# Two chained FFNs behind a recurrence: the 64-row matmul of the K = 320 remainder widened to 128 rows, and a re-scaled emission clock

## The chip, the cores and the metric

One core of one Trainium2 chip. The metric is device time in microseconds (us) of one execution. PE is TensorE (PEld its weight loads), DVE VectorE, ACT ScalarE, POOL GpSimd, SP SyncE.

## The reference, cut to what matters

A recurrence over 768 steps gives 3072 tokens of 320 numbers (the kernel's first 600 us; the change does not touch it). Then a router gives each token one of 8 experts (384 places each, greedily by the highest score), and two FFNs follow:

```python
for e in range(E):                       # E = 8, 384 tokens each
    h = np.maximum(x[mask] @ w1[e], 0.0) # [384, 320] @ [320, 1024]
    out[mask] = h @ w2[e]                # [384, 1024] @ [1024, 320]
h = x @ w_in                             # [3072, 320] @ [320, 2048]
g = h * np.clip(h + 3.0, 0.0, 6.0) / 6.0
return g @ w_out                         # [3072, 2048] @ [2048, 320]
```

## The kernel before, in words

**Stages.** `attention` is the recurrence. `moe` then does, for each of 8 experts in an order found at run time, both FFNs for its 384 tokens: 8 `hstage` (first FFN in, one 128-wide block of F1 each) with 8 `ystage` (first FFN out) two blocks behind, then 16 `gstage` (second FFN in) with 16 `ostage` (second FFN out) two blocks behind. The last two `ostage` of an expert, the scaling and the three scatters are done as `tails` between the first blocks of the next expert.

**Precision.** Every operand is a pair of float32r tiles, `h` (rounded) and `l` (what was lost). A product is h·h + l·h + h·l. `proj` (line 1091) does one block of the contraction over 320 for `hstage` and `gstage`: rows 0 to 127 (k = 0), 128 to 255 (k = 1), and the rest of 64 rows (k = 2). For the rest, one tile `x2` (or `y2`) holds h in its partitions 0 to 63 and l in 64 to 127, and the high weights `wh[2]` hold the same 64 rows twice, so that one matmul on 128 rows does h·h and h·l. A second matmul, on 64 rows, does l·h: `wl[2][0:64]` by `x2[0:64]`. So `proj` is 8 matmuls, in the order k = 0 (three), k = 2 (two), k = 1 (three), one 64-row matmul among seven on 128 rows; there are 8 + 16 blocks in each of 8 experts, 192 in all. In the page they are all line 1053 (`mm`), and the weights tell them apart: `x,w1l` and `y,win_l` are the 64-row ones.

**What sets the order.** Each engine runs its instructions in the order in which the program emits them. The routing of the next expert (`routing`, `place`, `xt`) is a set of Python generators that runs in between: `mm` emits a matmul and then calls `tick(n / 2400)`, with n its columns, so 0.16 for 384 columns and 0.133 for 320. This is the emission clock. A `yield r` in a generator means: go on when the clock has run r + PACE further (0.7). `later(us, f)` puts small steps (`gl` of a block, a weight DMA) off by so much of the clock. No time of the chip enters: if a DVE answer is not there when PE reaches the matmul that reads it, PE waits.

**The routing of an expert**, on DVE and PE by turns: six rounds of a search (DVE masks L774 and L776, 24 small matmuls L779, compare L793, matmul L796 on 8 rows, count L800); then matmuls L823 to L825, DVE, L840 and L841, then DVE L844 to L854, which end with `r_cb` (L852), and the matmuls L857 and L859 on `r_cb`, with `yield 1.8` between; then `place` (L907, L928) and `xt` (L1067).

**Other names.** `ph` is the PSUM tile of a projection (two of them, by turns), freed in `hstage` by DVE's `gl` (L1132) and in `gstage` by DVE's `gt` (L1206). POOL does the low parts (`w1l`, `w2b`, `w2c`, the second FFN's `gl`) and issues the gathers and scatters.

Of the kernel before, what the change touches and what calls it, by code (L numbers as in the profile page):

```python
# [18 lines left out]
F32, F32R, BF, I32 = mybir.dt.float32, mybir.dt.float32r, mybir.dt.bfloat16, mybir.dt.int32  # L19
AF = mybir.ActivationFunctionType  # L20
OP = mybir.AluOpType
# [583 lines left out]
E, CAP, NT, N = 8, 384, 24, 3072  # L605
DM, F1, F2 = 320, 1024, 2048
BIG = 1.0e38
PACE = 0.7
DVN, DVP = 4, 0
PACE1 = 0.3  # L610
NPRE = 8
# [18 lines left out]


def decoder(nc, raw_in, pool, wd):
    """One piece of w_in and w_out: from the float64's two words to the nearest float32."""
    V, A, P_, SY = nc.vector, nc.scalar, nc.gpsimd, nc.sync
    raws = {}

    def fetch(n):
        raw = raws[n] = pool.tile([128, 256, 2], I32, name="d_raw", bufs=2)
        SY.dma_start(raw.rearrange("p a b -> p (a b)"), raw_in[n].bitcast(I32))

    def head(n):
        raw = raws[n]
        w, lo = raw[:, :, 1], raw[:, :, 0]
        t = pool.tile([128, 256], I32, name="d_t", bufs=1)
        V.tensor_scalar(t, w, 3, 0x3ffffff8, op0=OP.logical_shift_left, op1=OP.bitwise_and)
        hf = pool.tile([128, 256], I32, name="d_hf", bufs=1)
        V.scalar_tensor_tensor(hf, w, -(1 << 30), t, op0=OP.bitwise_and, op1=OP.bitwise_or)
        raws[n] = (w, t, hf, lo)

    def scale(n):  # L650
        w, ex, hf, lo = raws[n]
        lf = pool.tile([128, 256], F32, name="d_lf", bufs=1)
        A.mul(lf, lo.bitcast(mybir.dt.uint32), 2.0 ** -52)
        sp = pool.tile([128, 256], I32, name="d_sp", bufs=1)
        V.tensor_scalar(sp, hf, -(1 << 23), None, op0=OP.bitwise_and)
        V.tensor_scalar(ex, w, 20, 0x7ff, op0=OP.logical_shift_right, op1=OP.bitwise_and)
        raws[n] = (ex, hf, sp, lf)

    def add(n):
        ex, hf, sp, lv = raws[n]  # L660
        E = P_ if n % DVN < DVP else V
        E.tensor_mul(lv, lv, sp.bitcast(F32))
        E.tensor_add(lv, lv, hf.bitcast(F32))
        raws[n] = (ex, lv)

    def value(n):
        ex, lv = raws.pop(n)
        v = pool.tile([128, 256], F32, name="d_v", bufs=2)
        V.scalar_tensor_tensor(v, ex, 896.5, lv, op0=OP.is_ge, op1=OP.mult)
        SY.dma_start(wd[:, 256 * n:256 * n + 256], v)  # L670

    return NP, fetch, head, scale, add, value


def moe_consts(nc, per, io):
    """Constants and state of the routing: the tiles, and what fills them."""
    V, P_, SY = nc.vector, nc.gpsimd, nc.sync
    k = {}
    for n, shape, dt in (("rc", [128, 242], F32), ("iota", [128, 128], BF), ("io4", [128, 16], BF), ("io5", [128, 32], BF), ("io6", [128, 64], BF), ("iot", [128, 3], BF), ("ones", [128, 128], BF), ("tri", [128, 128], BF),
                         ("tri1", [128, 128], BF), ("rst", [128, E * NT], F32), ("asg", [128, NT, E], F32), ("unas", [128, NT], F32),  # L680
                         ("act", [128, E], F32), ("capb", [128, E], F32), ("q", [128, E], F32), ("q8", [128, 1], F32),
                         ("spacer", [128, 1], F32), ("three", [128, 1], F32)):
        k[n] = per.tile(shape, dt, name=n)
    rc = k["rc"]
    k["prefw"] = rc[:, 0:192].rearrange("p (j e) -> p j e", j=NT)
    k["jp"] = rc[:, 192:240].rearrange("p (j c) -> p j c", j=NT)
    k["pcol"] = rc[:, 240:241]

    def io_(n, w, base=0):
        P_.iota(k[n], pattern=[[1, w]], base=base, channel_multiplier=0, allow_small_or_imprecise_dtypes=True)  # L690

    fill = [lambda: SY.dma_start(rc, io["rc"]), lambda: io_("iota", 128), lambda: io_("iot", 3, -8)]
    fill += [lambda n=n, v=v: P_.memset(k[n], v) for n, v in (("ones", 1.0), ("rst", 1.0), ("asg", 0.0), ("unas", 1.0), ("act", 1.0), ("capb", BIG),
                                                             ("q", float(CAP)), ("q8", float(CAP)), ("three", 3.0))]
    fill += [lambda: P_.memset(k["rst"].rearrange("p (e j) -> p e j", e=E)[:, :, 0:1], 0.0)]
    fill += [lambda b=b: P_.tensor_scalar(k[f"io{b}"], k["iota"][:, :1 << b], 0.5 ** b, None, op0=OP.mult) for b in (4, 5, 6)]
    fill += [lambda: V.tensor_scalar(k["tri"], k["iota"], k["pcol"], None, op0=OP.is_gt),
             lambda: V.tensor_scalar(k["tri1"], k["iota"], k["pcol"], None, op0=OP.is_ge)]

    return k, fill  # L700


def moe(tc, nc, io, cst, xd, LG, wd, out):
# [5 lines left out]
    V, A, P_, T_, SY = nc.vector, nc.scalar, nc.gpsimd, nc.tensor, nc.sync  # L709
    ident = cst["ident"]  # L710
    k = cst["k"]
# [6 lines left out]
    def rt(shape, dtype, name, bufs=1):  # L718
        return wk.tile(shape, dtype, name="r_" + name, bufs=bufs)
# [3 lines left out]
    def routing(ph, vbits):  # L723
        S3, S2 = [128, NT, E], [128, NT]
        if ph < E - 1:
# [10 lines left out]
            s = rt(S2, I32, "s")  # L736
# [26 lines left out]
            for i, (sh, b) in enumerate(vbits):  # L763
# [16 lines left out]
                if i:  # L780
                    t = rt(S2, F32, "dp")
                    V.tensor_scalar(t, z, cnt, None, op0=OP.subtract)
                else:
                    t = z
# [67 lines left out]
            V.tensor_copy(cb, cn)  # L852
            V.tensor_sub(unas, unas, sel)
            V.tensor_add(asg, asg, oa)  # L854
            yield 1.8
            pn = ps.tile([128, 512], F32, name="pn")
            T_.matmul(pn[:, 0:E], ones, cb, start=True, stop=True)  # L857
            pc = ps.tile([128, 512], F32, name="pc")
# [83 lines left out]
        res[ph]["xg"] = xg  # L942
        yield XG

# [1 line left out]
    def stage(name):  # L946
        return wk.tile([128, 1024], F32, name="stg", bufs=2)

# [2 lines left out]
    wo_h = per.tile([128, 16, DM], F32R, name="wo_h")  # L951
    wo_l = per.tile([128, 16, DM], F32R, name="wo_l")

    def split(hi, lo, src, leng, rows=128):
        A.copy(hi, src)
        leng.tensor_tensor(lo[0:rows], src[0:rows], hi[0:rows].bitcast(F32), OP.subtract)

    rest = []

    def load_win():  # L960
        wh, wl = wo_h.rearrange("p k n -> p (k n)"), wo_l.rearrange("p k n -> p (k n)")
        cuts = [(win_h[:, k], win_l[:, k], 2048 * k, 1024 * c, 1024, k) for k in range(2) for c in range(2)]
        k2 = [(win_h[:, 2], win_l[:, 2], 4096, 1024 * c, 1024, 2) for c in range(2)]
        wo = [(wh, wl, 5120, c, n, 1) for c, n in ((0, 1280), (1280, 1280), (2560, 1536), (4096, 1024))]
        cuts += wo[:2] + k2 + wo[2:]
        for i, ((hi, lo, o, c, n, k), g) in enumerate(zip(cuts, (2, 2, 0, 0, 1, 1, 2, 1, 0, 2))):
            if g == 0:
                t = wk.tile([128, 4, 3, 128], F32, name="w1r", bufs=3).rearrange("p m k n -> p (m k n)")
            elif g == 1:
                t = wk.tile([128, 4, DM], F32, name="w2r", bufs=3).rearrange("p k n -> p (k n)")  # L970
            else:
                t = stage("win")
            if k == 2:
                for h in range(2):
                    SY.dma_start(t[64 * h:64 * h + 64, :n], wd[64 * (c // 1024):64 * (c // 1024) + 64, 4096:5120])
            else:
                SY.dma_start(t[:, :n], wd[:, o + c:o + c + n])
            f = lambda hi=hi[:, c:c + n], lo=lo[:, c:c + n], t=t[:, :n], r=64 if k == 2 else 128: split(hi, lo, t, P_, r)
            if i < NWIN:
                f()  # L980
            else:
                rest.append(f)
# [20 lines left out]
    R_ = {"cur": -1, "g": False, "w": [], "core": 0, "placed": 0, "hold": 0.0}  # L1003
    runs = []

    class Run:
# [4 lines left out]
        def tick(self, us):  # L1011
            self.have += us
            while self.have >= self.need:
                if self.guard is not None and not self.guard():
                    break
                self.have, self.need, self.guard = 0.0, 0.0, None
                r = next(self.gen, None)
                if r is None:
                    runs.remove(self)
                    break  # L1020
                if callable(r):
                    self.guard = r
                else:
                    self.need = r + (PACE if R_["core"] > 1 else PACE1)

    late = []

    def later(us, f):
        late.append([us, f])

    def flush():
        while late:
# [18 lines left out]

    def mm(o, l, r, n, **kw):
        T_.matmul(o, l, r, **kw)  # L1053
        tick(n / 2400.0)

    def xt(ph):
        xg = res[ph]["xg"]
# [32 lines left out]
    def proj(p, wh, wl, x):  # L1090
        xh, xl, x2 = x
        for k in (0, 2, 1):
            if k == 2:
                mm(p, wh[2], x2, CAP, start=False, stop=False)
                mm(p, wl[2][0:64], x2[0:64], CAP, start=False, stop=False)
                continue
            mm(p, wh[k], xh[:, k], CAP, start=(k == 0), stop=False)
            mm(p, wl[k], xh[:, k], CAP, start=False, stop=False)
            mm(p, wh[k], xl[:, k], CAP, start=False, stop=(k == 1))
# [300 lines left out]
```

## Time and profile before

| what | us |
|---|---|
| runs | 1319.57, 1326.3, 1359.72 |
| median | 1326.3 |
| span of the profiled execution | 1309.5 |
| PE busy in the span | 1176.6 |
| one expert, from one L857 to the next | 90.4 |
| PE busy in it | 87.5 |

The span runs from the first to the last instruction of one profiled execution. What lies around it is 10.1 us to the fastest run (1319.57 - 1309.5) and 16.8 us to the median. A view that groups instructions gives busy time and the mean duration of one; because matmuls overlap, the distance between the starts of two in a row tells what one costs, and not its duration.

### The profile page before, as it was taken

Reading aid. Unit: us, or ns where it says so; the run is one execution under the profiler, and the core shown is the slowest. Engines: PE = TensorE matmul, PEld = TensorE weight load, DVE = VectorE, ACT = ScalarE, POOL = GpSimd, SP = SyncE. Lnnn points to the kernel's source line nnn. Section 1 sums busy time; section 2 is a strip of 40 time slices with the busy share of each in tenths; the row PEclk is TensorE's granted clock in tenths of the full one; section 3 lists DMA queues with packets and bytes.
Section 4 is the critical chain, followed back from the end, with each engine's and each line's share of the span. In section 5 each row is a group of like instructions: output and inputs, shape, how many; then the busy total and the mean of one; then the engine's idle time right before and its main releaser. Section 6 shows DMA issues by size and latency. Waiting matters only on the chain.

```text
span 1309.5 us, 30652 instructions
## 1 busy us (share of the span) xinstructions
PE 1176.6 (90%) x11921; PEld 995.9 (76%) x11921; DVE 896.1 (68%) x2200; ACT 598.6 (46%) x1430; POOL 698.6 (53%) x1142
## 2 busy tenths in 40 slices
PE   4398999999999999516999999999999999999996
PEld 4278889888898887414787887887887878888886
DVE  7989998888986766896688757657557564342221
ACT  5656666556664565412324334343343333443432
POOL 4277876677665751255346435435444455383632
PEclk7689998778985899857999999999999999999999
DMA  6467666667665364613020200301101102021000
GB/s 155 102 135 175 169 161 152 136 151 167 143 151 127 82 136 115 194 40 104 1 94 21 99 11 16 101 4 57 63 6 55 60 12 104 6 75 45 17 1 16
DMA packets 179372, 113.20 MB, mean 86 GB/s; under 512 B 132124, under 2 KB 160540, under 8 KB 179228
## 3 DMA queue, kind: packets, MB, share of 16 engines
q1 hardware_dynamic: 172316, 80.31, 26.0%
q0 software_dynamic: 6912, 30.94, 6.9%
q8 instruction: 94, 1.54, 0.5%
q14 instruction: 50, 0.41, 0.1%
HBM read 91.81 MB, written 19.40 MB: 85 GB/s over the span
## 4 chain that ended last, share of the span: by engine, by line
PE 73%; DVE 20%; issue 3%; ACT 2%; DMA 1%; POOL 0%; SPq 0%; DVEq 0%; POOLq 0%; ACTq 0%
PE ph L1053 27%; PE acc L1053 19%; PE pA L210 3%; PE pF L368 2%; PE pc L779 2%; PE pH L300 2%; PE pE L309 2%; PE pC L322 2%; PE pG L377 2%; PE pD L331 2%; DVE r_mk L774 2%; PE pC L402 2%; PE pE L349 1%; DVE abd L178 1%; PE pG L380 1%
## 5 line engine op out<-in xcount | busy, mean ns | idle before, releaser
L1210 POOL TENSOR_TENSOR gl<-gt,gh 128x384 fp32r<-128x384 f32 x112 | 120.9, 1080 | 242.5 <-ACT gh L1207 216.2
L268 POOL TENSOR_TENSOR ttmp<-ttw,pin 128x126 f32<-128x126 f32 (+25 forms) x341 | 149.3, 438 | 104.9 <-DMA td<-ttw 41.1
L1206 DVE SCALAR_TENSOR_TENSOR gt<-gu,ph 128x384 f32<-128x384 f32 (+1 forms) x130 | 71.0, 546 | 170.8 <-ACT gu L1203 170.8
L270 POOL TENSOR_TENSOR ttw<-ttw,ttmp 128x126 f32<-128x126 f32 (+25 forms) x341 | 159.5, 468 | 26.7
L1203 ACT ACTIVATE gu<-ph,three 128x384 f32<-128x384 f32 (+1 forms) x130 | 74.8, 577 | 177.0 <-PE ph L1053 176.5
L1053 PE MATMUL acc<-wo_h,gh 128*128 128x320 f32 x384 | 120.3, 313 | 0.0
L1053 PE MATMUL acc<-wo_h,gl 128*128 128x320 f32 x384 | 119.9, 312 | 0.0
L1053 PE MATMUL acc<-wo_l,gh 128*128 128x320 f32 x384 | 119.6, 312 | 0.0
L1207 ACT CAST gh<-gt 128x384 fp32r<-128x384 f32 (+1 forms) x130 | 66.0, 508 | 95.0 <-DVE gt L1206 92.6
L1053 PE MATMUL ph<-yh,win_h 128*128 128x384 f32 x256 | 100.8, 394 | 0.0
L1106 POOL TENSOR_TENSOR w1l<-w1r,w1h 128x384 fp32r<-128x384 f32 x64 | 69.0, 1084 | 54.3 <-ACT w1h L1105 53.1
L1053 PE MATMUL ph<-yl,win_h 128*128 128x384 f32 x256 | 87.6, 342 | 0.7 <-DVE yl L1185 0.7
L1053 PE MATMUL ph<-yh,win_l 128*128 128x384 f32 x256 | 87.6, 342 | 0.0
L774 DVE SCALAR_TENSOR_TENSOR r_mk<-io,r_cnt,r_dz 128x384 bf16<-128x384 bf16 (+3 forms) x84 | 82.5, 1012 | 1.4
L1132 DVE SCALAR_TENSOR_TENSOR gl<-ph,gh 128x384 fp32r<-128x384 f32 x64 | 35.5, 554 | 66.7 <-ACT gh L1131 66.7
L210 PE MATMUL pA<-abd,kb 128*128 128x128 f32 x336 | 59.6, 331 | 22.9 <-POOL abd L178 13.4
L1053 PEld LDWEIGHTS acc<-wo_h,gh 128*128 128x128 f32 x384 | 72.2, 188 | 1.3 <-issue 0.8
L1053 PEld LDWEIGHTS acc<-wo_h,gl 128*128 128x128 f32 x384 | 72.1, 188 | 0.5 <-issue 0.2
L1053 PEld LDWEIGHTS acc<-wo_l,gh 128*128 128x128 f32 x384 | 72.1, 188 | 0.2
L210 PEld LDWEIGHTS pA<-abd,kb 128*128 128x128 f32 x336 | 50.4, 230 | 25.3 <-POOL abd L178 14.0
L1131 ACT ACTIVATE gh<-ph 128x384 fp32r<-128x384 f32 x64 | 31.5, 492 | 79.5 <-PE ph L1053 79.4
L1053 PEld LDWEIGHTS ph<-yh,win_h 128*128 128x128 f32 x256 | 47.9, 187 | 23.9 <-issue 23.6
(286 smaller groups left out, 3324.5 us busy)
## 6 DMA issues: line engine op xcount, KB each, us to landing
d_raw<-w SPq DMA_DIRECT2D x40, 256.0 KB
wx<-wx SPq DMA_DIRECT2D x24, 419.7 KB
kb<-kb SPq DMA_DIRECT2D x24, 416.0 KB
vu<-vr SPq DMA_DIRECT2D x24, 416.0 KB
vp<-v SPq DMA_DIRECT2D x48, 160.0 KB
pin<-pd SPq DMA_DIRECT2D x24, 256.0 KB
wd<-d_v SPq DMA_DIRECT2D x40, 128.0 KB
xd<-xrow SPq DMA_DIRECT2D x48, 80.0 KB
```

The costliest lines, as they stand in the source:

```text
L210: T_.matmul(p[:, g], kb[:, g], abd[:, g], start=True, stop=True)
L268: out.append((eng, lambda eng=eng, a=a, e=e, t=t, r=r, m=m: eng.tensor_mul(t, tt[:, a:e, r:r + 1].to_broadcast([128, e - a, m]), pin[:, r: ...
L270: out.append((eng, lambda eng=eng, a=a, e=e, t=t, r=r: eng.tensor_sub(tt[:, a:e, r + 1:], tt[:, a:e, r + 1:], t)))
L774: V.scalar_tensor_tensor(mk[:, sl], bc(io[:, None, :], sh3), cnt, bc(z[:, sl, None], sh3), op0=OP.add, op1=OP.is_le)
L1053: T_.matmul(o, l, r, **kw)
L1106: P_.tensor_tensor(l, w1[m], h.bitcast(F32), OP.subtract)
L1131: A.activation(hh, p, AF.Relu)
L1132: later(L0, lambda: V.scalar_tensor_tensor(hl, p, 0.0, hh.bitcast(F32), op0=OP.max, op1=OP.subtract))
L1203: A.activation(u[:, c], p[:, c], AF.Relu, bias=three, scale=1.0)
L1206: V.scalar_tensor_tensor(t[:, c], u[:, c], 6.0, p[:, c], op0=OP.min, op1=OP.mult)
L1207: A.copy(gh[:, c], t[:, c])
L1210: (V if m >= GLV else P_).tensor_sub(gl[:, c], t[:, c], gh[:, c].bitcast(F32))
```

## The change

1. In `proj` the l·h matmul of the rest takes all 128 rows: `wl[2]` by `x2`. The lower 64 rows add l·l, which is below float32. So that `wl[2]` is filled there, the split of w_in's rest now writes 128 partitions instead of 64 (two POOL instructions in the whole kernel); for w1 it did already.
2. The clock runs 0.013 more for each matmul (0.173 for 384 columns, 0.146 for 320), and delays are multiplied by 1.08, with PACE 0.64 instead of 0.7.
3. The yield ahead of L857 is 4.0 instead of 1.8.

```diff
-PACE = 0.7
+PACE = 0.64
+MMX = 0.013
+SC = 1.08
@@ routing
             V.tensor_add(asg, asg, oa)
-            yield 1.8
+            yield 4.0
             pn = ps.tile([128, 512], F32, name="pn")
             T_.matmul(pn[:, 0:E], ones, cb, start=True, stop=True)
@@ load_win
-    def split(hi, lo, src, leng, rows=128):
+    def split(hi, lo, src, leng):
         A.copy(hi, src)
-        leng.tensor_tensor(lo[0:rows], src[0:rows], hi[0:rows].bitcast(F32), OP.subtract)
+        leng.tensor_tensor(lo, src, hi.bitcast(F32), OP.subtract)
-            f = lambda hi=hi[:, c:c + n], lo=lo[:, c:c + n], t=t[:, :n], r=64 if k == 2 else 128: split(hi, lo, t, P_, r)
+            f = lambda hi=hi[:, c:c + n], lo=lo[:, c:c + n], t=t[:, :n]: split(hi, lo, t, P_)
@@ Run.tick, later, mm
-                    self.need = r + (PACE if R_["core"] > 1 else PACE1)
+                    self.need = SC * (r + (PACE if R_["core"] > 1 else PACE1))
-        late.append([us, f])
+        late.append([SC * us, f])
-        tick(n / 2400.0)
+        tick(n / 2400.0 + MMX)
@@ proj
                 mm(p, wh[2], x2, CAP, start=False, stop=False)
-                mm(p, wl[2][0:64], x2[0:64], CAP, start=False, stop=False)
+                mm(p, wl[2], x2, CAP, start=False, stop=False)
```

The change moves instructions as well. The line numbers of the kernel after are 2 higher. On DVE, in the routing done during the fourth expert, from `r_cb` (L852, after it L854) on; `gl` is the evacuation of a block of the first FFN, and `q` (L861) reads what the matmul L857 wrote. Before:

```order
L852 CAST r_cb<-r_cn 128x8 [waits DVE_49]
L853 TENSOR_TENSOR unas<-unas,r_sel 128x24
L854 TENSOR_TENSOR asg<-asg,r_oa 128x192
L1132 SCALAR_TENSOR_TENSOR gl<-ph,gh 128x384 [waits Activation_49]
L861 TENSOR_TENSOR q<-q,pn 128x8 [waits PE_49]
```

And after:

```order
L854 CAST r_cb<-r_cn 128x8 [waits DVE_49]
L855 TENSOR_TENSOR unas<-unas,r_sel 128x24
L856 TENSOR_TENSOR asg<-asg,r_oa 128x192
L1134 SCALAR_TENSOR_TENSOR gl<-ph,gh 128x384 [waits Activation_49] x2
L863 TENSOR_TENSOR q<-q,pn 128x8 [waits PE_49]
```

One block of the first FFN more lies between `r_cb` and its use, and both `gl` stand behind `r_cb` in DVE's queue.

On PE, the same place: L857 with what stands around it, before:

```order
L1053 MATMUL acc_13594<-gl,w2c 64x384
L857 LDWEIGHTS ones
L857 MATMUL pn<-r_cb,ones 128x8 [waits DVE_49]
L859 LDWEIGHTS r_cb
L859 MATMUL pc<-ones,r_cb 8x1
L1053 MATMUL acc_13592<-gh,w2a 128x384
```

And after:

```order
L1055 MATMUL ph<-xh,w1h 128x384 [waits DVE_49]
L859 LDWEIGHTS ones
L859 MATMUL pn<-r_cb,ones 128x8
L861 LDWEIGHTS r_cb
L861 MATMUL pc<-ones,r_cb 8x1
L1055 MATMUL ph<-xh,w1l 128x384 [waits Pool_49]
```

Between L841 and L857 there are 21 matmuls of the FFNs before and 33 after here (21 before in all routings from the third expert on, 29 to 35 after in all); the last of them after the change is the first matmul of a projection, which waits for its `ph`, that is for a `gl` behind `r_cb`.

## Rows read from the trace of the kernel before

**Rows 1.** The page: span, the chain's shares by line.

```profile
span 1309.5 us, 30652 instructions
PE ph L1053 27%; PE acc L1053 19%; PE pA L210 3%; PE pF L368 2%; PE pc L779 2%; PE pH L300 2%; PE pE L309 2%; PE pC L322 2%; PE pG L377 2%; PE pD L331 2%; DVE r_mk L774 2%; PE pC L402 2%; PE pE L349 1%; DVE abd L178 1%; PE pG L380 1%
```

**Rows 2.** Windows: length, busy PE, PEld, DVE, ACT, POOL, clock; sum of ten that cover the span.

```profile
0.00:600.00 600.00, 494.35 (x7514) 430.83 (x7515) 503.09 (x1213) 339.94 (x852) 360.94 (x738) 0.82 0.58 138
804.90:895.30 90.40, 87.51 (x592) 72.03 (x592) 58.53 (x151) 32.32 (x72) 43.17 (x51) 0.98 0.13 44
804.90:811.00 6.10, 6.08 (x25) 5.10 (x25) 3.18 (x14) 1.44 (x4) 2.50 (x5) 0.72 0.07 30
...
sum 1310.00, PE 1176.57 PEld 995.85 DVE 896.06 ACT 598.55 POOL 698.59; mean PE 117.66 PEld 99.59 DVE 89.61 ACT 59.86 POOL 69.86
```

**Rows 3.** Line 1053 by form: count, ns min/median/max, first and last start, rows*columns.

```profile
L1053 PE MATMUL ph<-y,win_l x128: 435/436/443, 644.5 to 1294.2; 64*128 64x384 f32 x128
L1053 PE MATMUL ph<-x,w1l x64: 435/441/687, 612.2 to 1244.2; 64*128 64x384 f32 x64
```

**Rows 4.** PE's timeline through one projection: start, us, engine, line, names, rows*columns.

```profile
706.99 0.33 PE L1053 MATMUL ph<-xl,w1h 128*128 128x384 f32 x1
707.16 0.34 PE L1053 MATMUL ph<-x,w1h 128*128 128x384 f32 x1
707.43 0.44 PE L1053 MATMUL ph<-x,w1l 64*128 64x384 f32 x1
707.80 0.44 PE L1053 MATMUL ph<-xh,w1h 128*128 128x384 f32 x1
708.08 0.34 PE L1053 MATMUL ph<-xh,w1l 128*128 128x384 f32 x1
708.26 0.34 PE L1053 MATMUL ph<-xl,w1h 128*128 128x384 f32 x1
```

**Rows 5.** PE's timeline at a routing matmul on 8 rows, and a 64-column one.

```profile
633.13 0.20 PE L796 MATMUL pn<-r_ge,ones 8*128 8x64 bf16 x1
633.26 0.44 PE L1053 MATMUL ph<-xl,w1h 128*128 128x384 f32 x1
633.54 0.33 PE L1053 MATMUL acc<-gh,w2c 128*128 128x384 f32 x1
633.71 0.34 PE L1053 MATMUL acc<-gl,w2c 128*64 128x384 f32 x1
633.89 0.35 PE L1053 MATMUL acc<-gh,w2a 128*128 128x384 f32 x1
```

**Rows 6.** Waits from 645 to 1300 us: who for whom, total us, times, longest.

```profile
PEld ph L1053 <- issue: 75.5, 351, 0.4
PE pn L857 <- DVE r_cb L852: 11.0, 4, 2.8
```

**Rows 7.** PE's timeline at a wait for `r_cb`; idle before and its releaser in brackets.

```profile
797.83 0.17 PE L841 MATMUL pn<-r_flb,tri 128*128 128x24 bf16 x1
...
804.92 0.17 PE L857 MATMUL pn<-r_cb,ones 128*128 128x8 bf16 x1 [2.76 <-DVE r_cb L852]
...
806.29 0.41 PE L1053 MATMUL ph<-xh,w1h 128*128 128x384 f32 x1
...
809.91 0.33 PE L1053 MATMUL acc<-gh,w2a 128*128 128x384 f32 x1
```

**Rows 8.** DVE's timeline ahead of that L857.

```profile
799.87 1.98 DVE L845 TENSOR_TENSOR r_sel<-r_sel,r_gt 128x24 f32<-128x24 f32 x1
...
803.49 1.38 DVE L852 CAST r_cb<-r_cn 128x8 bf16<-128x8 f32 x1
```

**Rows 9.** POOL's timeline just then.

```profile
799.47 1.01 POOL L1251 DMA_INDIRECT out_dram<-stg,r_idx  x1
```

**Rows 10.** DVE's timeline at a search round.

```profile
841.57 0.23 DVE L793 TENSOR_SCALAR r_ge<-pc,q 8x32 bf16<-8x32 f32 x1
```

**Rows 11.** PE's timeline at that round.

```profile
841.86 0.17 PE L796 MATMUL pn<-r_ge,ones 8*128 8x32 bf16 x1
```

## The prediction

> **What bounds the kernel now.** I read the page first: the span is 1309.5 us, PE is busy for 1176.6 of it [rows 2], and in the chain that ended last the two costliest entries are line 1053, the matmuls of both FFNs, with 27% and 19% [rows 1]. Then the windows by stage. Up to 600 us (the recurrence) PE and DVE are about equally busy, and nothing there is edited. One expert, from one L857 to the next, takes 90.40 us with PE busy for 87.51; DVE has 58.5, POOL 43.2, ACT 32.3 [rows 2]. So in the FFN stage, some 690 us of the span, PE's queue is the bound, and what one matmul costs there is the distance to the next start.
>
> The forms of line 1053 and a timeline give that distance. In a projection the starts stand 0.17 to 0.18 us apart, but not around the 64-row matmul: it starts 0.27 after the one ahead of it, the next starts 0.37 after it, and the one after that 0.28 later [rows 4]. From the third matmul of k = 0 to the third of k = 1 that is 1.27 us for five distances, where five ordinary ones (0.175) make 0.875. **Each projection loses 0.395 us around its one 64-row matmul.** There are 128 + 64 of them, all with a median of 435 to 441 ns [rows 3]; the high-weight matmul ahead reads the same moving tile on 128 rows and lasts 0.34 [rows 4].
>
> Why it loses time is told by two more views. The weight loads of the projections wait 75.5 us for nothing that the profile shows ("issue"), 351 times [rows 6]: about two for each of the 183 projections in that window, 0.41 us for each projection, the same loss seen from the weights' side. And another matmul that uses few rows, the search's L796 on 8, has the same mark: after it 0.13, then 0.28 to the next, and that next one lasts 0.44; a matmul with 64 columns and 128 rows has none (0.17 before it, 0.18 behind it) [rows 5]. So a change of the number of rows is what costs, once on entry and once on return.
>
> **What the change does, part by part.**
>
> *A, the 128-row matmul.* It takes the loss away: the new one has the rows, columns and moving tile of the high-weight matmul ahead of it, so I price it at 0.175. Gain: 192 x 0.395 = 76 us from the starts, 183 x 0.41 = 75 from the weight loads. A few of the 192 have a routing matmul between them and their neighbours and will keep a part of the loss, so I take 74, with 70 and 76 as bounds, and 0 if rows are not the cause (a rival below). The split of w_in's rest on 128 partitions instead of 64 is the same two POOL instructions with the same 1024 elements in each partition, once in the kernel; I cost it at nothing, covered by the routing of the first expert, in which PE mostly waits for DVE (bound: 2 us, two POOL instructions of about 1.0 [rows 9], if they were twice as long and nothing covered them).
>
> The Trainium skill, "TensorE: Matmul & The Clock Gate", in the table of "Why this matters for your kernels", says that a single matmul on 32 rows takes the same time as one on 128. By that rule alone A would be 0 and the sum further on 1299.5 us; by the starts it is 74 and 1225.5. The trace differs from it: the rule may hold for the columns streamed, but the distances around the 64-row matmul are longer [rows 4].
>
> *B, the wait for `r_cb`.* In four experts PE stands 2.76 us before L857, 11.0 in all [rows 6, 7]. Behind it the clock falls: 0.72 granted over 6.1 us, a stretch of it at 1.2 GHz [rows 2]. From 806.29 to 809.91 PE needs 3.62 us for ten distances that hold one 64-row matmul, where 10 x 0.175 + 0.39 = 2.14 would do: 1.5 us more, 6 in four experts [rows 7]. From L841 to L857 are 7.1 us, of which 21 matmuls fill 4.3. DVE's part is long because two tiny instructions take 1.98 and 1.38 us [rows 8], where another tiny one takes 0.23 [rows 10]; POOL was issuing a scatter when the first began [rows 9]. After the change there are 29 to 35 matmuls instead of 21. At 0.175, 33 are 5.8 us, so with the same DVE chain 1.3 us of wait is left. If DVE's two instructions are not held up, it is none; if the routing matmul L841, which can now stand up to eight matmuls earlier against the block whose `gl` DVE does first, makes the chain start later, it is 2.1. I take 1.0. It may not be shown at L857: the projection ahead of it needs a `gl` that DVE has queued behind `r_cb`, so PE may stand there. I take it that the clock then stays up; the rows show its fall only behind 2.76 us. Gain: 4 x (2.76 - 1.0) + 6 = 13 us; bounds 0 (the wait and the low clock stay) and 17.
>
> *C, the new clock.* In matmuls of 384 columns a delay r was (r + 0.7)/0.16 and is 1.08(r + 0.64)/0.173 = (r + 0.64)/0.16: 0.4 matmul less for each yield, and for `later` the same. So the routing keeps its place among the matmuls, except L857's 12 more. What changes is time: each distance between a routing matmul and the one that needs DVE's answer shrinks by 0.395 us for each projection in it. Most answers came early enough. The tightest is in a search round: L793 ended at 841.80 [rows 10] and L796 started at 841.86 [rows 11]. What is late next is this kind: some 0.2 us more in each of five experts, 1 us, and I add 2 for the two experts ahead of them, whose routing is packed closer. I cost C at 3 us, with bounds 0 and 10 (some 0.28 us in each of 36 search rounds, 6 in each of 6 routings).
>
> *Sum*, against the profiled execution's own span: 1309.5 - 74 - 13 + 3 = 1225.5 us. What lies around the span was 10.1 us to the fastest run and 16.8 to the median, so 1235.6 to 1242.3. I take **1240 us**. In one expert: 90.4 - 24 x 0.385 - 1.8 - 1.5 + 0.2, about 78 us.
>
> **The rivals.**
>
> *The chain gives part of it back.* A holds, but the waits for DVE grow as PE comes sooner: the 11 us and the low clock stay (B = 0), and the rounds lose C's upper 10. For it: DVE is busy for 58.5 of 90.4 us, which would be 58.5 of some 80, and its tiny instructions are held up at times that the order cannot show. Against it: most waits in the trace have room. 1309.5 - 74 + 10 = 1245.5, so 1256 to 1262 us. Chance 0.15.
>
> *The change does not do what it says.* If the 64-row matmul were slow for what surrounds it (its weights' tile, say) and not for its rows, A would be 0 and B and C would stay: 1309.5 - 13 + 3 = 1299.5, so 1310 to 1316 us, within 2% of 1326.3. For it: the trace has no case of the same weights on 128 rows. Against it: L796, with other weights and another type, shows the mark as well, and on few rows too [rows 5]. Chance 0.05. The page named under A would end here.
>
> *Slower.* DVE's answers become the bound in the search rounds: L793 and L800 come behind a `gt` or a mask in DVE's queue, PE stands at L796 and L779, and the clock falls behind each wait. There are 6 rounds in each of the 6 routings that lie beside experts, 36. To eat A's 74 us each would have to cost 2.1 us; for 2% slower than 1326.3 it takes 26 us more, 2.8 us each, with B lost as well (the longest wait now is 2.76, and not in a round). At 3 us a round: 1309.5 - 74 + 108 = 1343.5, so 1354 to 1360 us. Chance 0.02; the round of [rows 10, 11] is at most 0.2 us from having room.
>
> **How the numbers follow.** The forecast has 0.78. Its own range: 1309.5 - 76 - 17 = 1216.5 to 1309.5 - 70 - 6 + 6 = 1239.5, with 10.1 and 16.8 around it 1227 to 1256. The range given reaches over the first rival, 1225 to 1264; the other two, 0.07, lie outside, as do the tails. A measurement of this kernel can tell about 2% from no change (1300 to 1353 count as the same). Faster: 0.78 + 0.15 = 0.93; same 0.05; slower 0.02.
>
> **What would show each step.** A: in the form view all of `x,w1l` and `y,win_l` read 128*128 at about 338 ns, the starts in a projection stand 0.17 to 0.18 apart throughout, and the weight loads' "issue" wait falls from 75.5 us to under 10 (L796 and L779 keep theirs). B: the wait for L852 is gone or under 1.5 us at L857 or at the `ph` ahead of it, and the clock is 1.00 in the stretch behind. C: PE's waits for L793, L774 or L837 add up to a few microseconds. The forecast is wrong if the 0.37 after the second k = 2 matmul stays (A), or if PE's idle time in an expert is above 4 us (the first rival).

## The result, and the profile after

| | before | after |
|---|---|---|
| median of 6 runs, us | 1322.93 | 1262.69 |
| lowest and highest | 1309.9 to 1359.72 | 1251.35 to 1272.42 |
| ratio, 95% interval | | 0.9553, 0.9478 to 0.9629 |
| span of the profiled execution | 1309.5 | 1263.6 |
| first FFN matmul starts at | 610.7 | 625.8 |
| stretch of the eight experts | 688.9 | 627.8 |
| PE idle in it | 14.3 | 21.1 |

The ratio is taken over each kernel's faster runs, so it is not quite that of the two medians. The kernel is faster by 4.5%, within the stated range of 1225 to 1264, 1.3 us under its upper end: 1262.7 for a forecast of 1240. The stretch of the experts (here and below: from the start of the first FFN matmul to the end of the last, read from PE's timeline) is 61.1 us shorter. The span fell by 45.9 only, because the recurrence ahead of it, which has the same instructions in the same order, took 15 us longer in this execution; the section on the hardware comes back to that.

The timeline of PE through one projection after the change, to set beside [rows 4]:

```profile
885.34 0.34 PE L1055 MATMUL ph<-xl,w1h 128*128 128x384 f32 x1
885.51 0.33 PE L1055 MATMUL ph<-x,w1h 128*128 128x384 f32 x1
885.68 0.33 PE L1055 MATMUL ph<-x,w1l 128*128 128x384 f32 x1
885.86 0.33 PE L1055 MATMUL ph<-xh,w1h 128*128 128x384 f32 x1
886.03 0.33 PE L1055 MATMUL ph<-xh,w1l 128*128 128x384 f32 x1
886.20 0.33 PE L1055 MATMUL ph<-xl,w1h 128*128 128x384 f32 x1
```

Five distances take 0.86 us, where they took 1.27. Part A's other two signs are there as well: the former 64-row matmuls read 128*128, with medians of 336 and 334 ns instead of 436 and 441, and the "issue" wait of the projections' weight loads falls from the 75.5 us of [rows 6] to 0.4 in the same window. Of the form view, and of the waits:

```profile
L1055 PE MATMUL ph<-y,win_l x128: 333/336/522, 657.2 to 1248.5; 128*128 128x384 f32 x128
L1055 PE MATMUL ph<-x,w1l x64: 334/334/525, 627.3 to 1204.6; 128*128 128x384 f32 x64
PEld ph L1055 <- issue: 0.4, 2, 0.2
```

Windows of the profile after: the first, second and fourth expert and the last. Columns as in [rows 2].

```profile
625.80:715.00 89.20, 82.48 (x674) 72.73 (x674) 69.70 (x185) 32.83 (x75) 39.93 (x45) 0.97 0.12 39
715.00:801.50 86.50, 82.23 (x597) 75.40 (x595) 59.61 (x158) 30.85 (x70) 41.33 (x51) 0.95 0.14 46
881.50:960.80 79.30, 77.88 (x594) 71.44 (x593) 58.62 (x151) 32.04 (x72) 41.64 (x51) 1.00 0.14 50
1184.50:1253.60 69.10, 69.10 (x420) 67.85 (x418) 19.05 (x39) 32.10 (x74) 33.18 (x45) 1.00 0.02 8
```

Before, by the same marks, these four took 92.7, 86.2, 90.3 and 78.5 us. The last, with no routing beside it, gained 9.3, which is what 24 x 0.39 makes. The fourth gained 10.9. But the second gained nothing, with PE idle for 4.3 us and its clock at 0.95, and the first 3.5, with PE idle for 6.7.

What PE waited for in the stretch of the experts (waits: who for whom, total us, times, longest), the largest:

```profile
PE acc L1055 <- DVE stg L1242: 3.6, 2, 2.0
PE pn L842 <- DVE r_exf L837: 2.5, 1, 2.5
PE px L1069 <- DMA xg<-xd,r_idx: 2.5, 2, 1.5
PE ph L1055 <- DVE yl L1187: 2.3, 4, 0.9
PE px L930 <- DVE r_oz L926: 1.6, 3, 0.8
```

The 11.0 us for `r_cb` of [rows 6] are gone, and many smaller waits stand in their place; PE is idle for 21.1 us in all.

### The profile page after: what moved, and what is told of

It is laid out like the page before. It is cut to its first block, busy times and chain, and to the rows that moved or that the text cites. A ratio compares the mean times of both kernels' runs of the same rounds, so it can differ in the third digit from the quotient of the medians.

```text
span 1263.6 us, 30649 instructions
## 1 busy us (share of the span) xinstructions
PE 1122.8 (89%) x11917; PEld 1013.1 (80%) x11921; DVE 898.5 (71%) x2200; ACT 597.0 (47%) x1430; POOL 688.8 (55%) x1142
## 4 chain that ended last, share of the span: by engine, by line
PE 62%; DVE 26%; issue 3%; ACT 3%; DMA 2%; POOL 2%; SPq 0%; DVEq 0%; POOLq 0%; ACTq 0%
PE ph L1055 18%; PE acc L1055 15%; PE pA L210 3%; PE pF L368 3%; PE pC L322 2%; PE pE L309 2%; PE pG L377 2%; PE pD L331 2%; PE pH L300 2%; PE pc L781 2%; PE pC L402 2%; PE pE L349 2%; DVE r_mk L776 2%; PE pG L380 2%; PE pB L232 1%
## 5 line engine op out<-in xcount | busy, mean ns | idle before, releaser
L270 POOL TENSOR_TENSOR ttw<-ttw,ttmp 128x126 f32<-128x126 f32 (+25 forms) x341 | 155.5, 456 | 26.8 <-POOL ttmp L268 0.2
L1055 PE MATMUL ph<-yh,win_h 128*128 128x384 f32 x256 | 88.6, 346 | 0.0
L1055 PE MATMUL ph<-yh,win_l 128*128 128x384 f32 x256 | 87.8, 343 | 0.0
L210 PE MATMUL pA<-abd,kb 128*128 128x128 f32 x336 | 60.5, 335 | 25.4 <-POOL abd L178 14.6
L776 DVE SCALAR_TENSOR_TENSOR r_mk<-io,r_cnt,r_dz 128x384 bf16<-128x384 bf16 (+3 forms) x84 | 76.4, 943 | 1.4
L1134 DVE SCALAR_TENSOR_TENSOR gl<-ph,gh 128x384 fp32r<-128x384 f32 x64 | 35.2, 552 | 46.2 <-ACT gh L1133 45.9
L781 PEld LDWEIGHTS <-r_ohu 128*8 128x8 bf16 x1032 | 30.7, 85 | 46.1 <-issue 44.3
L368 PE MATMUL pF<-rbd,vu 128*128 128x128 f32 x384 | 63.8, 317 | 0.0
```

The source lines that it names most:

```text
L210: T_.matmul(p[:, g], kb[:, g], abd[:, g], start=True, stop=True)
L270: out.append((eng, lambda eng=eng, a=a, e=e, t=t, r=r: eng.tensor_sub(tt[:, a:e, r + 1:], tt[:, a:e, r + 1:], t)))
L368: T_.matmul(p[:, g], vu[:, g], o[:, g], start=True, stop=True)
L776: V.scalar_tensor_tensor(mk[:, sl], bc(io[:, None, :], sh3), cnt, bc(z[:, sl, None], sh3), op0=OP.add, op1=OP.is_le)
L781: T_.matmul(pc[0:E, :K], ohu[:, j], mk[:, j], start=(j == 0), stop=(j == NT - 1))
```

## The experiments

Theory going in: the loss belongs to a change of the number of rows; what is missing from the forecast are waits, because a faster PE reaches the routing's matmuls before DVE has the answers. Rival: the new clock puts the routing in worse places. As runs of one kernel scatter by some 3% with the recurrence, the stretch of the experts in the profile is compared beside the ratio. It comes from one profiled execution of each kernel, in which the experts begin anywhere from 610.7 to 646.2 us; only the change was profiled twice (e10: 628.3 us and 627.8).

| kernel | ratio to before, interval | experts, us | PE idle in it |
|---|---|---|---|
| before | 1 | 688.9 | 14.3 |
| the change | 0.9553, 0.9478 to 0.9629 | 627.8 | 21.1 |
| e1: 128 rows alone | 0.971, 0.9582 to 0.9838 | 627.3 | 20.9 |
| e2: clock and yield alone | 1.0024, 0.9954 to 1.0093 | 682.4 | 9.7 |
| e3: 64-row matmul in two halves | one run, 1352.56 us | 698.6 | 12.4 |
| e4: 128 rows and yield | 0.9602, 0.9477 to 0.9728 | 628.3 | 22.8 |
| e5: change, yield 4.0 from the third routing | 0.9507, 0.94 to 0.9614 | 625.9 | 20.2 |
| e6: e5, L796 on 128 rows | 0.9552, 0.9445 to 0.9659 | 621.0 | 21.1 |
| e7: e1, scatters later | 0.9353, 0.9221 to 0.9486 | 605.7 | 6.4 |
| e8: e6, scatters later | 1221.12 to 1262.1 us, no interval | 612.7 | 11.9 |
| e9: e7, L796 on 128 rows | 0.9358, 0.9301 to 0.9414 | 600.8 | 6.9 |
| e10: the change once more | 0.9619, 0.9553 to 0.9685 | 628.3 | 20.8 |
| e11: before, scatters later | one run, 1295.8 us | 670.1 | 2.8 |

### e1 and e2: the two halves of the change apart

```diff
 # e1, against before (and the split of w_in's rest on all rows)
-                mm(p, wl[2][0:64], x2[0:64], CAP, start=False, stop=False)
+                mm(p, wl[2], x2, CAP, start=False, stop=False)
 # e2, against after
-                mm(p, wl[2], x2, CAP, start=False, stop=False)
+                mm(p, wl[2][0:64], x2[0:64], CAP, start=False, stop=False)
```

> Only the 128-row matmul; the clock, PACE and the yield of 1.8 stay as before, and with them the order of all instructions. Theory (the change of rows costs 0.39 us a projection; what went missing are waits for VectorE, because PE now reaches the routing's matmuls sooner): the last expert, which has no routing beside it, takes 69.1 us as in the changed kernel (78.4 before); the wait for r_cb grows from 2.76 to about 3.2 us with the low clock behind it; the stretch of the eight experts takes about 632 us (688.9 before, 627.8 after the change). Rival (the new clock is what makes the waits, and the rows alone give their whole 74 us): about 615 us, and a ratio of 0.945 or less.

> Only the new clock (MMX, SC, PACE) and the yield of 4.0, with the 64-row matmul kept: the order of the changed kernel at the old speed of PE. Theory (new waits come from PE being faster, not from the new places): the wait at L857 is gone, few new ones, the stretch of the experts about 675 us (688.9 before), ratio about 0.99. Rival (the new places make the waits): waits of 15 to 20 us in sum as in the changed kernel, and about 690 to 700 us.

The rows alone gave the whole gain of the stretch: 627.3 us against 627.8 of the full change; the intervals of the two ratios overlap. The last expert took 69.2. On the timeline of PE the wait for `r_cb` grew from 2.76 to 3.37 us, and behind it a matmul of 384 columns lasts 0.69 instead of 0.34, which is the low clock (0.72 granted from 803.9 to 810.0):

```profile
803.93 0.17 PE L857 MATMUL pn<-r_cb,ones 128*128 128x8 bf16 x1 [3.37 <-DVE r_cb L852]
804.03 0.17 PE L859 MATMUL pc<-ones,r_cb 128*8 128x1 bf16 x1
804.12 0.69 PE L1053 MATMUL acc<-gh,w2a 128*128 128x384 f32 x1
```

The clock and the yield alone gave 6.5 us of the stretch and nothing that the ratio can tell: 3 to 5 us each in the third, fourth and sixth expert, under 1 in the fifth, and 3 us lost in each of the first two (95.9 and 89.0 against 92.7 and 86.2), where L857 now lies 15 and 20 matmuls later. So neither side is right alone. At the old speed the new places already cost in the first two experts (the rival), and at the new speed both sets of places make 21 us of waits (the theory).

### e3: is it the matmul or the change of rows?

```diff
-                mm(p, wl[2][0:64], x2[0:64], CAP, start=False, stop=False)
+                for c in (slice(0, 192), slice(192, 384)):
+                    mm(p[:, c], wl[2][0:64], x2[0:64, c], 192, start=False, stop=False)
```

> The kernel before with its 64-row matmul of 384 columns cut into two of 192 columns, one behind the other, on the same 64 rows and the same weights. If the loss belongs to a change of the number of rows (once in, once out), a projection takes at most 0.05 us more and the last expert 78.4 to 79.6 us. If it belongs to every 64-row matmul, each projection takes about 0.39 us more and the last expert about 87.5 us.

The last expert took 79.1 us against 78.5, 0.03 us for each projection. On PE's timeline both halves stand in one row, and what is around them is as before: 0.27 on entry, 0.39 for both halves together, 0.28 behind.

```profile
1300.63 0.33 PE L1053 MATMUL ph<-y,win_h 128*128 128x384 f32 x1
1300.90 0.46 PE L1053 MATMUL ph<-y,win_l 64*128 64x192 f32 x2
1301.29 0.45 PE L1053 MATMUL ph<-yh,win_h 128*128 128x384 f32 x1
1301.57 0.34 PE L1053 MATMUL ph<-yh,win_l 128*128 128x384 f32 x1
1301.75 0.34 PE L1053 MATMUL ph<-yl,win_h 128*128 128x384 f32 x1
```

A second 64-row matmul behind the first costs next to nothing: the price is that of the change, once in and once out. Whether the matmul itself or its weight load pays it is not told apart: before the change the load of a 128-row matmul starts 0.17 us ahead of its matmul, and that of the 64-row one only with it (707.43 in [rows 4]).

```profile
706.99 0.19 PEld L1053 LDWEIGHTS ph<-x,w1h 128*128 128x128 f32 x1
707.43 0.18 PEld L1053 LDWEIGHTS ph<-x,w1l 64*128 64x128 f32 x1 [0.25 <-issue]
```

The whole stretch of e3 is 9.7 us longer than before, which the halves do not explain: its second expert alone takes 11.3 us more, with PE idle for 2.5 us and a granted clock of 0.90; what brought that about was not tried. The Trainium skill, "TensorEngine Tiling (Array Packing)", Key Properties, says that changing the tiling mode drains TensorE while changing the tile does not; the rows of e3 fit that, with 0.39 us for the pair of changes.

### e4 and e5: the yield and the clock

```diff
 # e4, against e1
-            yield 1.8
+            yield 4.0
 # e5, against after
-            yield 4.0
+            yield 4.0 if ph > 2 else 1.8
```

> The 128-row matmul and the yield of 4.0, with the old clock (no MMX, no SC, PACE 0.7). Every routing then takes some 2.2 units of the clock more, so that it drifts about 14 matmuls later with each expert. Theory: no wait at L857, otherwise the waits of the rows-only kernel; the stretch of the experts about 618 us, a little better than the changed kernel's 627.8. Rival (the new clock places the routing better): 635 us or more, since the late routing runs into the forced end of an expert.

> The changed kernel with the yield of 4.0 only from the third routing on, 1.8 in the first two; all routing then lies 15 to 24 matmuls earlier than in the changed kernel. Theory (the longer yield pushes the first two routings to where the first expert's end is forced and into the scatters of the first expert, and that costs its gain): the first two experts take about 85.5 and 79 us as with the rows alone (89.2 and 86.4 in the changed kernel), the others about 80 as they do, and the stretch of the experts about 617 us (627.8). Rival (PE's speed alone makes those waits): no gain in the first two, 625 us or more.

Both missed. e4 gave 628.3, not 618: the wait at L857 went, and others came, 22.8 us in all. e5 gave 87.8 and 81.8 us in the first two experts, better than the 89.2 and 86.4 of the change, worse than the 85.5 and 79.1 of e1; and the routings that followed, now 21 matmuls earlier, found a new place to wait (7.0 us at the matmul L907, in four experts). Four placements of the same routing (the change, e1, e4, e5) end within 2.4 us of each other, with 20 to 23 us of waits each. Moving the routing along PE's queue moved the waits and did not remove them, which points to something else that holds DVE up.

### e7: what holds DVE up

On DVE's timeline of the kernel after, ahead of the 2.5 us wait at 730.43:

```profile
724.75 0.36 DVE L830 TENSOR_TENSOR r_ft<-pn,q 128x192 f32<-128x192 f32 x1 [0.18 <-PE pn L827]
725.15 3.02 DVE L831 TENSOR_TENSOR r_ft<-r_ft,r_oe 128x192 f32<-128x192 f32 x1
728.21 0.35 DVE L833 TENSOR_REDUCE r_fl<-r_ft 128x24 f32<-128x192 f32 x1
728.59 1.57 DVE L835 TENSOR_TENSOR_SCAN r_cumf<-r_fl 128x24 f32<-128x24 f32 x1
```

L831 and L830 have the same shape and take 3.02 and 0.36 us; the shortest L831 of this profile takes 0.48. POOL's timeline of the same microseconds:

```profile
724.76 1.03 POOL L1253 DMA_INDIRECT out_dram<-stg,r_idx  x1 [0.16 <-DVE gl L1134]
725.82 1.04 POOL L1108 TENSOR_TENSOR w1l<-w1r,w1h 128x384 fp32r<-128x384 f32 x1
726.80 0.33 POOL L1118 TENSOR_TENSOR w2c<-w2r,w2c 128x64 fp32r<-128x64 f32 x1
727.08 0.74 POOL L1119 TENSOR_TENSOR w2b<-w2r,w2a 128x256 fp32r<-128x256 f32 x1
727.76 0.09 POOL L1252 MEMSET spacer<- 128x1 f32 x1
728.01 1.04 POOL L1253 DMA_INDIRECT out_dram<-stg,r_idx  x1 [0.16 <-issue]
729.08 1.00 POOL L1108 TENSOR_TENSOR w1l<-w1r,w1h 128x384 fp32r<-128x384 f32 x1
```

POOL runs from 724.76 to 730.08 with hardly a gap; L831 ends at 728.17, and L835 at 730.16. Both begin while POOL issues a scatter, as `r_cb`'s L845 did in [rows 8, 9]. Moving the scatters tells whether they are the cause:

```diff
 # e7, against e1
-            tails.extend(lambda i=i: scatter(ot, i) for i in range(3))
+            sc.extend(lambda i=i: scatter(ot, i) for i in range(3))
         for m in range(16):
             gstage(m)
+            if m in (4, 5, 6) and sc:
+                sc.pop(0)()
...
```

> The rows-only kernel (order as before), with the three scatters of an expert issued in the next expert's gstages 4 to 6 instead of its hstages 2 to 4. Theory (VectorE's two tiny instructions ahead of r_cb are held up while GpSimd runs its weight splits and the scatters without a gap): they take about 0.2 us each instead of 1.98 and 1.38, the wait at L857 falls from 3.35 to under 1 us in four experts, the clock stays up there, and the stretch of the experts falls from 627.3 to about 611 us. Rival (the hold comes from the weight splits alone, or from VectorE itself): the wait stays above 2.5 us and the time within 3 us.

605.7 us, 22 less than e1, with the order of PE and of DVE untouched. The views of e7 (DVE's timeline ahead of L857, and the wait itself):

```profile
799.07 0.83 DVE L845 TENSOR_TENSOR r_sel<-r_sel,r_gt 128x24 f32<-128x24 f32 x1
799.93 0.18 DVE L846 TENSOR_TENSOR r_sel<-r_sel,unas 128x24 f32<-128x24 f32 x1
...
801.11 0.17 DVE L852 CAST r_cb<-r_cn 128x8 bf16<-128x8 f32 x1
```

```profile
801.33 0.17 PE L857 MATMUL pn<-r_cb,ones 128*128 128x8 bf16 x1 [0.37 <-DVE r_cb L852]
```

L845 is down from the 1.98 of [rows 8] to 0.83 and L852 from 1.38 to 0.17; in e1, L846 took 2.07 and L852 1.48. The 0.83 falls beside weight splits (a `w2b` at 798.05 and a `w1l` at 798.84), so these seem to hold DVE too, for shorter. PE idles 6.4 us in the whole stretch, and the third to fifth experts run at a clock of 1.00:

```profile
789.90:867.70 77.80, 77.30 (x594) 71.38 (x594) 57.88 (x152) 32.23 (x72) 43.06 (x51) 1.00 0.15 51
```

So the place of the scatters is the cause of most of the waits in e1's order (20.9 to 6.4 us of idle PE), and of about half in the change's (e6 to e8, further on: 21.1 to 11.9). How a scatter does it is not shown. It is not only that POOL runs without a gap: in e7 the weight splits do so too, from 796.10 to 801.11 with gaps of at most 0.11, and beside them only L845 is held, while L846 to L852 are not:

```profile
798.05 0.75 POOL L1117 TENSOR_TENSOR w2b<-w2r,w2a 128x256 fp32r<-128x256 f32 x1
798.84 1.02 POOL L1106 TENSOR_TENSOR w1l<-w1r,w1h 128x384 fp32r<-128x384 f32 x1
799.97 0.33 POOL L1116 TENSOR_TENSOR w2c<-w2r,w2c 128x64 fp32r<-128x64 f32 x1
800.26 0.85 POOL L1117 TENSOR_TENSOR w2b<-w2r,w2a 128x256 fp32r<-128x256 f32 x1
```

What the long holds of the change, e1 and e7 have in common is their beginning. Of DVE's instructions in the stretch 13, 15 and 13 run more than 1.0 us over the shortest time of the same instruction in these profiles, and each of them begins while POOL issues a scatter or a gather. (In e2, e3 and e4 seven such holds begin beside a weight split.) In e7 all 13 are beside gathers. Summed over the stretch, what DVE takes beyond those shortest times fell only from 75.4 us (e1) to 69.3: most of the holding moved from the steps that PE waits for to others.

The Trainium skill, "SBUF — State Buffer", Terms, says of the port pair that VectorE and GpSimd share that it is held for a full instruction and that the loser blocks. The times above fit that, save that a held instruction can wait for more than one of POOL's: L831 outlasted the end of a scatter and three splits.

### e11: what the rows are worth when nothing else waits

```diff
 # against before: the scatters as in e7
-            tails.extend(lambda i=i: scatter(ot, i) for i in range(3))
+            sc.extend(lambda i=i: scatter(ot, i) for i in range(3))
...
```

> The kernel before (64-row matmul, old clock) with the scatters moved as in e7. It differs from e7 by the 128 rows alone, with the wait for r_cb out of the way in both. Theory (the rows are worth 24 x 0.39 = 9.3 us in each expert, and what the rows-only kernel gave less was the longer wait and the low clock): each of the experts 2 to 4 takes 86 to 87 us (77.8 in e7, 90.4 before), the stretch of the experts about 676 to 680 us, 70 to 74 us more than e7. Rival (the rows are worth the 61 us that the rows-only kernel gained): about 667 us.

670.1 us: between the two sides. The windows of e11, its third expert and its last:

```profile
792.50:878.20 85.70, 85.70 (x594) 70.95 (x593) 57.64 (x151) 32.31 (x72) 43.33 (x51) 1.00 0.14 46
1205.60:1284.20 78.60, 78.53 (x420) 67.27 (x418) 19.14 (x40) 32.40 (x74) 33.23 (x46) 1.00 0.02 7
```

In the last expert the rows are worth 78.5 - 69.2 = 9.3 us (e11 against e7), in the third 85.7 - 77.8 = 7.9, after 0.5 given back to waits. In the fourth, the five distances around the former 64-row matmul shrank by 0.37 to 0.40 us in 19 of the 24 projections, and by 0.28, 0.20, 0.20, 0.12 and nothing in the other five: those have routing matmuls among their distances, or, the last, a wait. That is 1.2 us less than 24 full gains. Summed over all 192 projections these distances shrank by 69.0 us. The stretch fell by 64.4, and by 68 if the 3.6 us by which e7 waits longer are left out.

### e6, e8 and e9: the next matmul with few rows, and the clock again

```diff
 # e6, against e5: gez is a [128, 64] tile, zero but for its first 8 rows
-                ge = rt([128, K], BF, "ge")
-                V.tensor_scalar(ge[0:E], pc[0:E, :K], q8[0:E], None, op0=OP.is_ge)
+                V.tensor_scalar(gez[0:E, :K], pc[0:E, :K], q8[0:E], None, op0=OP.is_ge)
...
-                T_.matmul(pn[:, :K], ones[0:E, :], ge[0:E], start=True, stop=True)
+                T_.matmul(pn[:, :K], ones, gez[:, :K], start=True, stop=True)
```

> As e5, and the search's matmul L796 on 128 rows instead of 8, with rows 8 to 127 of its moving tile zero. Theory (the loss belongs to a change of the number of rows, whatever the matmul): 36 such matmuls beside the experts stop costing some 0.3 us each, so 9 to 11 us less than e5, about 607 us, and the matmul behind L796 lasts 0.34 instead of 0.44 us. Rival (it is a matter of the float32r weights): no difference to e5 beyond 3 us.

> e6 with the scatters moved as in e7: 128 rows throughout, the new clock, the late yield, the later scatters. Theory: the waits at the start of an expert go, about 600 us for the stretch of the experts, and a ratio of about 0.935 to the kernel before. Rival (the scatters hold up the gstages' own steps, GpSimd's gl among them): 607 us or more.

> e7 (128 rows, the order of before, later scatters) with L796 on 128 rows as in e6. In e6 the padded L796 cost 128 ns beyond its neighbours instead of 316 (in 3 and out 125, instead of 96 and 220), so 36 x 0.19 = 6.8 us less than e7: about 599 us for the stretch of the experts, against 605.7 in e7 and 627.8 in the changed kernel. Rival (the search is bound by VectorE's answers, and PE only waits longer): 604 us or more.

Medians over the L796 that stand among FFN matmuls: on 8 rows, 96 ns more than usual ahead of it, 115 to the next, 105 more behind that; on 128 rows 3, 40 and 85. The loss on entry is gone, and 0.19 us of 0.32 in all. The 85 that stay were taken in [rows 5] for the mark of few rows and are not; what they belong to was not tried. The stretch fell by 4.9 us in both pairs (625.9 to 621.0, 605.7 to 600.8), half of what e6's expectation said and near that of e9's.

e8 and e9 both have 128 rows everywhere and the later scatters; e8 has the new clock with the late yield, e9 the old order. 612.7 against 600.8, with 11.9 and 6.9 us of waits: with the scatters later, the old clock and yield are the better ones here. e8 missed its expectation of about 600 and lies on the rival's side (607 or more); the reason that the rival gives was not tested. e9 has the shortest stretch of all. Its runs take 1224.77 to 1246.79 us, median 1227.85, 32 us under the change's beside it (e10: 1259.9); its ratio cannot be told from e7's.

### e10: the change once more

> The changed kernel once more. Theory (executions differ in the recurrence alone, whose steps take 8.4 us or 14.6 us each, and the stretch of the experts repeats): 626 to 630 us for the experts, while the recurrence and the first routing end anywhere between 610 and 646 us. Rival (the 15 us that the changed kernel's profile lost before the experts belong to the change): the experts start at 622 to 629 us again, and the runs of before scatter less than those of after.

628.3 us of experts with PE idle for 20.8, and the same largest waits at the same places: this part repeats. Single experts repeat less well, to 2.3 us (86.4 and 84.2 for the second), so differences of that size in one expert say little. The experts began at 634.3, not at 625.8, and with the 64-row matmul at 614.1 (e11) and 642.3 (e3): the time ahead of them varies by itself.

## Why the prediction was right, and where it was not

**The number: in the range, with luck.** 1262.7 lies above the forecast's own range of 1227 to 1256. It is within the stated one because that was stretched over the first rival (1256 to 1262, chance 0.15). The sign that the prediction named for this rival, more than 4 us of idle PE in an expert, came in the first two (6.7 and 4.3 us).

**The bound and the mechanism: right.** PE's queue set the end, each projection lost 0.39 us around its 64-row matmul, and it went (e1, the last expert, the timeline). e3 shows that it belongs to the change of rows, and the rival in which A is 0 is out.

**A, 74 us: somewhat too high.** Measured between two kernels that differ by the rows alone and wait little (e11 and e7), A is 69.0 us at the projections themselves and 64 to 68 in the stretch, under its bounds of 70 and 76. The term that was mis-sized is "a few of the 192 have a routing matmul between them and their neighbours", set at 2 us: it is 1.2 us in an expert like the fourth and some 7 in all (192 x 0.395 - 69.0). The evidence from L796 was also read too widely: of its mark, 85 ns behind it stay on 128 rows.

**B, 13 us: right in its place, and not a gain in sum.** The wait for `r_cb` is gone, and the clock is 1.00 in the third to sixth expert. Against e1, which has the rows alone, the change is 9.8 us shorter in these four experts and 11.0 longer in the first two. What the step missed is in its own POOL row: the held-up instructions were taken for a property of that place. They go with POOL's scatters and weight splits at the start of every expert, and whatever part of the routing lies there can be held.

**C, 3 us: the step that failed most.** It was worked out from room in the search rounds. Of the 21 us of waits after, only 1.1 are for the answer of L793 (L795 after). The largest others are for L835 behind L831 (2.5, numbers of the kernel after), for the gathers and the `xt` at the first expert's forced end (some 4.6), for `stg` (3.6) and `yl` (2.3), and the clock falls to 0.97 and 0.95 in the first two experts. "The routing keeps its place among the matmuls, except L857's 12 more" was right for two routing matmuls in a row and wrong for the sum: the 2.2 units of the yield push every later step too, 13 to 15 matmuls in the first expert, toward its forced end and the next expert's scatters. PE's idle time went from 14.3 to 21.1 us instead of to some 10 (7 less by B, 3 more by C), as the rival "the chain gives part of it back" had it, but hardly in the rounds: about half of it goes with the place of the scatters (e6 to e8).

**The sum.** Forecast for the stretch of the experts: 74 + 13 - 3 = 84 us less; measured: 61.1. The rows give some 69 and the end of the `r_cb` waits and their low clock 17 to 19 (11 of waits and the prediction's 6 of clock; e11, where both are gone, gained 18.9). New waits take 18 back. The 7 to 9 us that are left are not split up here; the low clock in the first two experts is the likely part of them, as granted clocks of 0.97 and 0.95 over 89.2 and 86.4 us leave out some 7 us of full clock (an estimate from these four numbers).

**What lies around the span: wrongly named, and of little weight.** Each span is 1.7 us under its own run's time (1263.6 and 1265.33). The 10.1 and 16.8 us of the text compared the profiled execution with other executions, and that execution of before had the quickest way to the experts of all that were profiled (the FFNs begin at 610.7 us, elsewhere at 613.8 to 646.2). So they stand for the scatter of the recurrence. The miss is in the stretch: the median before less the measured 61.1 us is 1261.8, and the median after is 1262.7.

## What to carry to other kernels

Where a matmul on few rows stands among matmuls on 128, look at the distances between starts on both sides of it; if they are longer, fill the other rows (with zeros, or a term that is too small to matter): here the filled rows cost nothing (0.17 us from start to start). Before moving waiting steps along a queue, look at the durations of the instructions that answer them: if tiny ones take microseconds, see what another engine does beside them, and try moving that (e7: 22 us with PE's order untouched). A stage's own stretch in the trace, not the span, is what to set a sum against when another stage scatters.

## What the runs showed of the hardware

The recurrence, which no kernel here edits, and the first routing took between 611 and 646 us up to the first FFN matmul. The recurrence is done in 48 chunks of 16 steps, with one L370 on DVE in each. From one L370 to the next it is 7.3 to 10.7 us where the granted clock is 1.00 or near it, and 11.9 to 14.6 where it is near 0.50. Which chunks are slow differs from execution to execution: 8 of them in the profile of before and 11 in that of after, which is the 15 us between the two. The same window in the profiles of before and after:

```profile
120.00:180.00 60.00, 55.63 (x1031) 50.35 (x1027) 57.57 (x133) 41.77 (x113) 47.93 (x107) 1.00 0.69 164
```

```profile
120.00:180.00 60.00, 58.81 (x785) 53.25 (x782) 45.89 (x102) 32.32 (x87) 41.23 (x99) 0.69 0.57 131
```

1031 matmuls at a clock of 1.00, and 785 at 0.69, the mean of chunks at either level. In a slow chunk PE is at the low level of 1.2 GHz for about its whole length. Slow chunks come alone or up to four in a row (e1); what tips them was not tried.
